# Value block means made in the second unit of a batch and spread by GpSimd, with a 192-byte head pitch in the value tile

## The chip, the cores and the metric

The kernel runs on one core of a Trainium2 chip. The metric is device time in microseconds, the median of three runs. The profile is one profiled execution of the same program. The engines are PE (matrix products; its weight loads are shown apart as PEld), DVE (VectorE), ACT (ScalarE), POOL (GpSimd) and SP (which here only issues DMAs). Each engine works through its own instructions in order; they wait for each other on semaphores.

## The reference, cut to what matters

Four batches of block-sparse attention (8 heads, 768 positions, 64 features a head) feed a gated feed-forward layer with a residual gate.

```python
k_sum = k.reshape(B, H, nb, block, D).max(axis=3)      # 24 blocks of 32 positions
v_sum = v.reshape(B, H, nb, block, D).mean(axis=3)
scores_l = scale * q @ k.T          # kept where |i - j| < 16, else -1e9
scores_s = scale * q @ k_sum.T + log(block)
a = softmax(concat([scores_l, scores_s], -1))
x = a @ concat([v, v_sum], axis=2)                     # to [3072, 512]
g = x @ w_gate;  val = x @ w_val
ffn = (gelu(g) * val) @ w_out
out = x + sigmoid(x @ w_res) * ffn
```

So every query sees the 31 nearest keys and, for each of 24 blocks, the maximum of its keys and the mean of its values. The change concerns these means, `v_sum`.

## The kernel before, in words

The work is cut into 8 units, two halves (`half` 0 and 1) of 384 positions for each of 4 batches. While unit u goes through the feed-forward layer, its tail computes the attention of unit u + 1, so PE always has matrix products of both. A unit has two parts:

- the **fo loop**, 12 steps: eight matmuls each into g and vv (PSUM pool `ps_mm`, four buffers), GELU on ACT, the product gvT on DVE (`fo_step`, L293);
- the **tail**: for the next unit four pairs of heads through scores (`s_step`), exponential, mask, and the attention-value product (`av_step`, matmuls `ao` at L273), then four transposes (`xt_step`), between the output matmuls f of the present unit (`ffn_step`), its residual gate (`res_step`) and its output (`end_step`, which sends `out` on SP).

The order is written out by hand (`tc.manual_schedule()`), so each engine executes in the order of the code.

**The value tile.** `vext[b % 2]` holds, for each of 12 windows of 64 queries (t) and each head, 128 rows of keys by 65 columns: rows 0 to 95 are the 96 positions around the window, rows 96 to 127 the block means, 24 of them used, the same for every t. Columns 0 to 63 are the values, column 64 is one (it gives the softmax sum). Values come in by 12 DMAs on POOL's queue (`v_loads`). The tile of batch b is that of batch b - 2, so two batches exist at a time.

**The block means of batches 1 to 3** go through four steps. `vsum_grp` (L229): 12 matmuls (L233) of the averaging matrix `bgrp` with the values of the 12 windows, into a PSUM tile `vs` in pool `ps_t`, tag "t", which has one buffer and is shared with the transposes of `xt_step` and, for batch 1, of `k_step` and `q_step`. DVE copies it to `vpart` (L237). SP sends four small DMAs (L239) that bring the groups of six rows to rows 96 to 119 of `vsum`. Last, `vsum_bc` (L242) copies the rows of `vsum` into rows 96 to 127 of three windows of `vext` at a time, so four copies fill a batch. Before the change the matmuls stand in the tail of the first unit of the batch before (L420, unit 0, 2 or 4), and the four copies are on DVE in fo steps 0 to 3 of the unit that follows (L383, unit 1, 3 or 5). The first `av_step` that needs them is in that unit's tail. Batch 0 has its own way at the start (`vsum_mm`, then one copy of six windows on DVE and one on POOL, L344 and L345), and it stays.

**What else stands on these queues.** POOL issues the loads of batch b + 1 at the start of unit 2b (L369): batch 1 by `load_qk` and `v_loads`, batches 2 and 3 by `load_nat` (12 DMAs for k_nat, 6 for q_nat) and `v_loads`. The instructions stand on POOL back to back, and at most eight of its DMAs are in flight; k_nat and q_nat have one buffer each. SP transposes them into kW and qT (`turn_all`, after fo step 6 of units 2 and 4). For batch 1, PE transposes the keys and queries instead, one pair of heads a step, in fo steps 2 to 9 of unit 1 (`k_step`, `q_step`). On DVE the block maxima of the keys (`k_blocks`, L198 and L202) follow: in unit 1 with `k_step`, in units 3 and 5 in fo steps 4 to 7.

Of the kernel before, what the change touches and what calls it, by code (L numbers as in the profile page):

```python
# [9 lines left out]
BF16 = mybir.dt.bfloat16  # L10
# [5 lines left out]
def kernel(  # L16
# [11 lines left out]
    nc = tc.nc  # L28
    B, H, S, D = q.shape
# [10 lines left out]
    NT = S // QT  # L40
    HT = NT // 2
# [5 lines left out]
    NQ = S // 128  # L47
    PJ = 8
    PP = S // PJ

    const = ctx.enter_context(tc.tile_pool(name="const", bufs=1))
    wpool = ctx.enter_context(tc.tile_pool(name="wpool", bufs=1))
# [7 lines left out]
    ps_t = ctx.enter_context(tc.tile_pool(name="ps_t", bufs=1, space=bass.MemoryType.PSUM))  # L60
# [9 lines left out]
    qT = [const.tile([128, NQ, NP, 128], BF16, name=f"qT{i}") for i in range(2)]  # L70
    k_nat = const.tile([BAND, NT, DM], BF16, name="k_nat")
    q_nat = const.tile([128, NQ, DM], BF16, name="q_nat")
    vext = [const.tile([128, NT, H, D + 1], BF16, name=f"vext{i}") for i in range(2)]
    vsum = [const.tile([128, DM], BF16, name=f"vsum{i}") for i in range(2)]
    vpart = const.tile([128, DM], BF16, name="vpart")
    w_gate = wpool.tile([128, KO, DFF], BF16, name="w_gate")
# [4 lines left out]
    def load_qk(src, b, parts, name):  # L81
        t = qk.tile([PP, H, PJ, D], BF16, tag=name, name=name)
        hs = H // parts
        for i in range(parts):
            nc.gpsimd.dma_start(
                out=t[:, i * hs:(i + 1) * hs].rearrange("p h j d -> p h (j d)"),
                in_=src[b, i * hs:(i + 1) * hs].rearrange("h (p j) d -> p h (j d)", j=PJ),
            )
        return t
# [7 lines left out]
    def v_loads(b):  # L97
        for t in range(NT):
            r0, r1, src = v_window(b, t)
            nc.gpsimd.dma_start(out=vext[b % 2][r0:r1, t, :, 0:D], in_=src)  # L100
# [13 lines left out]
    def turn_all(b):  # L114
        nc.sync.dma_start_transpose(out=kW[b % 2].rearrange("d t g k -> d (t g) k")[:, :, 0:BAND],
                                    in_=k_nat.rearrange("p t f -> p (t f)"))
        nc.sync.dma_start_transpose(out=qT[b % 2].rearrange("d c g k -> d (c g) k"),
                                    in_=q_nat.rearrange("p c f -> p (c f)"))

    with tc.manual_schedule():  # L120
# [66 lines left out]
        def turn_pair(src, hp, pool, tag):  # L187
            tp = pool.tile([128, PJ, PP], BF16, tag=tag, name="tp")
            for j in range(PJ):
                for hh in range(2):  # L190
                    nc.tensor.transpose(tp[hh * 64:hh * 64 + 64, j, :], src[:, 2 * hp + hh, j, :],
                                        ident[0:PP, 0:PP])
            return tp

        def k_blocks(b, hp):
            kw = kW[b % 2][:, :, hp]
            ks = work.tile([128, NB], BF16, tag="ks", name="ks")
            nc.vector.tensor_reduce(  # L198
                out=ks.rearrange("d (t n) -> d t n", n=2),
                in_=kw[:, :, WIN:WIN + QT].rearrange("d t (n w) -> d t n w", w=BLK),  # L200
                axis=mybir.AxisListType.X, op=ALU.max)
            nc.vector.tensor_copy(kw[:, :, BAND:BAND + NB], ks.unsqueeze(1).to_broadcast([128, NT, NB]))  # L202

        def k_step(b, hp, pool, tag):
# [3 lines left out]
            src = bass.AP(tensor=tp.tensor, offset=tp[:, 0, 6:7].offset,  # L208
                          ap=[tp[:].ap[0], [8, NT - 2], [1, 12], [PP, PJ]])
            nc.scalar.copy(kw[:, 1:NT - 1, 0:BAND].rearrange("d t (p j) -> d t p j", j=PJ), src)  # L210
            nc.vector.tensor_copy(kw[:, 0, WIN:BAND].rearrange("d (p j) -> d p j", j=PJ),
                                  tp[:, :, 0:10].rearrange("d j p -> d p j"))
            nc.vector.tensor_copy(kw[:, NT - 1, 0:BAND - WIN].rearrange("d (p j) -> d p j", j=PJ),
                                  tp[:, :, PP - 10:PP].rearrange("d j p -> d p j"))
            k_blocks(b, hp)
# [13 lines left out]
        def vsum_grp(b, pool, tag):  # L229
            vs = pool.tile([128, DM], F32, tag=tag, name="vs")  # L230
            for i in range(3):
                for g in range(4):
                    nc.tensor.matmul(vs[32 * g:32 * g + 32, :], bgrp[:, i, :],  # L233
                                     vext[b % 2][0:BAND, 3 * g + i, :, 0:D],
                                     start=(i == 0), stop=(i == 2), tile_position=(0, 32 * g),
                                     skip_group_check=True)
            nc.vector.tensor_copy(vpart[:], vs[:])  # L237
            for g in range(4):
                nc.sync.dma_start(out=vsum[b % 2][96 + 6 * g:102 + 6 * g, :],  # L239
                                  in_=vpart[32 * g:32 * g + 6, :])  # L240

        def vsum_bc(b, lo, hi, eng):  # L242
            src = vsum[b % 2][96:128, :].rearrange("p (h d) -> p h d", d=D)
            src = src.unsqueeze(1).to_broadcast([32, hi - lo, H, D])
            eng.tensor_copy(vext[b % 2][96:128, lo:hi, :, 0:D], src)  # L245
# [19 lines left out]
        def av_step(u, hp, st, pool=ps_o, tag="ao"):  # L265
            b, half = u // 2, u % 2
            P = st["P", hp]
            ao = pool.tile([128, NSUB, 2, D + 1], F32, tag=tag, name="ao")
            for sub in range(NSUB):
                for hh in range(2):  # L270
                    for e in range(2):
                        t = 2 * sub + e
                        nc.tensor.matmul(ao[64 * e:64 * e + 64, sub, hh, :], P[:, hh, t, :],  # L273
                                         vext[b % 2][:, half * HT + t, 2 * hp + hh, :],
                                         start=True, stop=True, skip_group_check=True)
            rz = work.tile([128, NSUB, 2, 1], F32, tag="rz", name="rz")
            nc.vector.reciprocal(rz[:], ao[:, :, :, D:D + 1])  # L277
            xn = st["xn"].rearrange("p s (h d) -> p s h d", d=D)[:, :, 2 * hp:2 * hp + 2, :]
            nc.vector.tensor_mul(xn, ao[:, :, :, 0:D], rz.to_broadcast([128, NSUB, 2, D]))  # L279
# [86 lines left out]
        for u in range(NU):  # L366
            b, half = u // 2, u % 2
            nb = b + 1
            if half == 0 and nb < B:  # L369
                if nb == 1:  # L370
                    k_sb[nb] = load_qk(k, nb, 1, "k_sb")
                    q_sb[nb] = load_qk(q, nb, 1, "q_sb")
                    v_loads(nb)
                else:
                    load_nat(nb)
                    v_loads(nb)
            gvT = upool.tile([128, FO, TU], BF16, tag="gvT", name="gvT")
            for fo in range(FO):
                fo_step(st, gvT, fo)
                if half == 0 and 1 < nb < B and fo == 6:  # L380
                    turn_all(nb)
                if half == 1 and nb < B:
                    if fo < 4:  # L383
                        vsum_bc(nb, 3 * fo, 3 * fo + 3, nc.vector)
                    if nb == 1:
                        if 2 <= fo < 2 + NP:
                            k_step(nb, fo - 2, ps_t, "t")
                        elif 2 + NP <= fo < 2 + 2 * NP:
                            q_step(nb, fo - 2 - NP, ps_t, "t")
                    elif 4 <= fo < 4 + NP:  # L390
                        k_blocks(nb, fo - 4)
            n = u + 1
            if n < NU:
                nst = new_unit()
                s_step(n, 0, nst)
            else:
                nst = None
            res_step(st, 0)
            ffn_step(st, gvT, 0, 0, FO)
            if nst:  # L400
                av_step(n, 0, nst)
                s_step(n, 1, nst)
            end_step(u, st, 0)
            res_step(st, 1)
            ffn_step(st, gvT, 1, 0, 4)
            if nst:
                av_step(n, 1, nst)
                s_step(n, 2, nst)
            ffn_step(st, gvT, 1, 4, FO)
            if nst:  # L410
                av_step(n, 2, nst)
                s_step(n, 3, nst)
                xt_step(n, 0, nst, ps_t, "t")
            end_step(u, st, 1)
            res_step(st, 2)
            ffn_step(st, gvT, 2, 0, 4)
            if nst:
                av_step(n, 3, nst)
                xt_step(n, 1, nst, ps_t, "t")
            if half == 0 and nb < B:  # L420
                vsum_grp(nb, ps_t, "t")
            ffn_step(st, gvT, 2, 4, FO)
            if nst:
                xt_step(n, 2, nst, ps_t, "t")
                xt_step(n, 3, nst, ps_mm, "mm")
            end_step(u, st, 2)
            st = nst
# [30 lines left out]
```

## Time and profile before

| | |
|---|---|
| time, median of 3 runs | 305.78 us (303.92 to 307.77) |
| profiled execution, span | 302.2 us |
| around the span, against the median | 3.6 us |
| PE busy | 263.6 us, 87% of the span |
| DVE / ACT / POOL busy | 171.8 / 124.8 / 89.9 us |
| mean matmuls L233, idle of PE before them | 10.6 us in all |
| four copies L245 on DVE, batches 1 to 3 | 12 of 952 ns |
| one copy L245 on POOL, batch 0 | 2744 ns for six windows |

The profiled execution's own time is not given apart from its span; what lies around the span is taken as the difference to the median of the runs. In a row of the groups the idle time is that of the engine just before the group's instructions, with what ended most of it behind an arrow. In a row of a timeline the first number is the start, the second the time that the row spans; x12 says that 12 instructions are merged, and square brackets give the idle time before and what ended it. Line numbers are those of the kernel before; behind the change they are one higher from line 50 on.

### The profile page before, as it was taken

How to read it: one execution, taken by the hardware profiler on the slowest of the kernel's cores; microseconds unless marked ns; L12 is line 12 of the kernel's file. 1: busy time of each engine (PE TensorE's matmuls, PEld its weight loads, DVE VectorE, ACT ScalarE, POOL GpSimd, SP SyncE). 2: the span in 40 equal slices, each digit the busy share in tenths (PEclk: the TensorE clock that was granted, in tenths of full speed). 3: DMA queues.
4: the chain of work that ended last, by engine and by line, in shares of the span. 5: the costliest groups of instructions: out<-in, count | busy, mean ns of one | idle time of the engine just before them, and what ended most of it. 6: DMA issues, size and time to landing. Idle time of an engine off the chain costs nothing.

```text
span 302.2 us, 5706 instructions
## 1 busy us (share of the span) xinstructions
PE 263.6 (87%) x2307; PEld 144.4 (48%) x2330; DVE 171.8 (57%) x373; ACT 124.8 (41%) x188; POOL 89.9 (30%) x127
## 2 busy tenths in 40 slices
PE   1666999927889999997979999997999999999994
PEld 0623565502445455543535456553554556455641
DVE  3545643630994475447497584366994754475423
ACT  2652535420356643364224443543336433643310
POOL 7977683278970000579700000000000000000000
PEclk9978699985999999999999999999999999999999
DMA  6999999999999017999990019501100100010001
GB/s 102 167 101 187 196 206 207 165 158 134 155 116 52 0 72 144 173 122 171 161 44 2 35 37 198 100 35 38 38 2 0 69 37 2 1 72 35 2 36 69
DMA packets 98122, 27.51 MB, mean 91 GB/s; under 512 B 83688, under 2 KB 95024, under 8 KB 98096
## 3 DMA queue, kind: packets, MB, share of 16 engines
q0 software_dynamic: 79008, 16.85, 92.3%
q1 hardware_dynamic: 19088, 10.30, 13.4%
q8 instruction: 18, 0.29, 0.4%
q14 instruction: 8, 0.07, 0.1%
HBM read 33.69 MB, written 6.29 MB: 132 GB/s over the span
## 4 chain that ended last, share of the span: by engine, by line
PE 64%; DMA 13%; DVE 12%; issue 4%; ACT 3%; POOL 1%; SPq 1%; DVEq 0%; POOLq 0%
PE f L321 17%; PE g L297 16%; PE vv L301 15%; DMA q_sb<-in_q_dram 8%; PE r L311 6%; DVE vext L245 3%; DVE gvT L305 3%; PE ao L273 3%; DMA vext<-in_v_dram 3%; PE s L255 3%; DMA vsum<-vpart 3%; DVE ks L198 2%; PE xp L284 2%; SPq L239 1%; PE wp L342 1%
## 5 line engine op out<-in xcount | busy, mean ns | idle before, releaser
L304 ACT ACTIVATE ge<-g 128x384 f32<-128x384 f32 x96 | 47.2, 491 | 104.9 <-PE g L297 63.7
L297 PE MATMUL g<-xT,w_gate 128*128 128x384 bf16 x384 | 81.0, 331 | 1.6 <-DVE gvT L305 1.6
L301 PE MATMUL vv<-xT,w_val 128*128 128x384 bf16 x384 | 78.7, 328 | 1.7 <-DVE gvT L305 0.8
L305 DVE TENSOR_TENSOR gvT<-ge,vv 128x384 bf16<-128x384 f32 x96 | 52.6, 551 | 48.0 <-PE vv L301 47.6
L321 PE MATMUL f<-w_out,gvT 128*128 128x512 bf16 x274 | 66.9, 386 | 2.0 <-issue 1.8
L301 PEld LDWEIGHTS <-w_val 128*128 128x128 bf16 x384 | 37.7, 98 | 29.2 <-issue 5.5
L297 PEld LDWEIGHTS <-w_gate 128*128 128x128 bf16 x384 | 37.2, 99 | 26.7 <-issue 4.4
L321 PEld LDWEIGHTS <-gvT 128*128 128x128 bf16 x288 | 27.5, 99 | 34.0 <-issue 3.7
L259 ACT ACTIVATE P<-s,bias_t 128x768 bf16<-128x768 f32 x32 | 28.9, 903 | 34.2 <-PE s L255 34.1
L100 POOL DMA_DIRECT2D vext<-in_v_dram x48 | 36.6, 778 | 16.4 <-DMA w_out<-in_moe_w_out_dram 4.3
L262 DVE TENSOR_TENSOR P<-P,maskt 128x768 bf16<-128x768 bf16 x32 | 17.7, 554 | 21.2 <-ACT P L259 21.2
L108 POOL DMA_DIRECT2D k_nat<-in_k_dram x24 | 18.1, 762 | 36.8 <-DMA kW<-k_nat 32.9
L311 PE MATMUL r<-w_res,xT 128*128 128x512 bf16 x88 | 24.4, 381 | 0.4
L326 DVE SCALAR_TENSOR_TENSOR th<-th,f 128x512 f32<-128x512 f32 x24 | 16.3, 679 | 7.0 <-PE f L321 7.0
L279 DVE TENSOR_TENSOR xn<-ao,rz 128x384 bf16<-128x384 f32 x32 | 17.8, 557 | 1.1
L314 ACT ACTIVATE th<-r 128x512 f32<-128x512 f32 x24 | 14.3, 595 | 8.8 <-PE r L311 8.3
L328 DVE SCALAR_TENSOR_TENSOR o<-th,xn 128x512 f32<-128x512 f32 x24 | 16.6, 692 | 0.8
L273 PEld LDWEIGHTS <-P 128*64 128x64 bf16 x384 | 8.9, 113 | 14.4 <-DVE P L262 5.9
L198 DVE TENSOR_REDUCE ks<-kW 128x24 bf16<-128x768 bf16 x16 | 15.2, 949 | 0.3
L277 DVE RECIPROCAL rz<-ao 128x6 f32<-128x6 f32 x32 | 6.1, 192 | 15.7 <-PE ao L273 15.6
L245 DVE COPY vext<-vsum 32x1536 bf16<-32x1536 bf16 (+1 forms) x13 | 12.4, 952 | 4.1 <-DMA vsum<-vpart 3.8
L255 PE MATMUL s<-qT,kW 64*128 64x64 bf16 x384 | 11.4, 194 | 3.2 <-ACT P L259 3.2
(72 smaller groups left out, 177.7 us busy)
## 6 DMA issues: line engine op xcount, KB each, us to landing
out_dram<-o SPq DMA_DIRECT2D x24, 256.0 KB
vext<-in_v_dram POOLq DMA_DIRECT2D x40, 96.0 KB, 7.4
k_nat<-in_k_dram POOLq DMA_DIRECT2D x20, 96.0 KB, 5.4
w_gate<-in_moe_w_gate_dram POOLq DMA_DIRECT2D x6, 256.0 KB, 8.9
w_val<-in_moe_w_val_dram POOLq DMA_DIRECT2D x6, 256.0 KB, 9.2
w_out<-in_moe_w_out_dram POOLq DMA_DIRECT2D x3, 512.0 KB, 13.9
q_nat<-in_q_dram POOLq DMA_DIRECT2D x12, 128.0 KB, 5.8
k_sb<-in_k_dram POOLq DMA_DIRECT2D x2, 384.0 KB, 5.5
```

Of the source, the lines that this page charges most:

```text
L100: nc.gpsimd.dma_start(out=vext[b % 2][r0:r1, t, :, 0:D], in_=src)
L108: nc.gpsimd.dma_start(out=k_nat[r0:r0 + hi - lo, t].rearrange("p (h d) -> p h d", d=D), in_=k[b, :, lo:hi, :].rearrange("h p d -> p h d"))
L198: nc.vector.tensor_reduce(out=ks.rearrange("d (t n) -> d t n", n=2), in_=kw[:, :, WIN:WIN + QT].rearrange("d t (n w) -> d t n w", w=BLK), ...
L245: eng.tensor_copy(vext[b % 2][96:128, lo:hi, :, 0:D], src)
L255: nc.tensor.matmul(s[:, hh, t * QT:(t + 1) * QT], kw[ps, tt, hp, :], qt[ps, tt // 2, hp, (tt % 2) * QT:(tt % 2 + 1) * QT], start=True, sto ...
L259: nc.scalar.activation(P.rearrange("p a t q -> p a (t q)"), s[:, :, 0:TU], AF.Exp, scale=scale, bias=bias_t[:])
L297: nc.tensor.matmul(g[:, 0:TU], w_gate[:, ko, fs], st["xT"][:, ko, :], start=(ko == 0), stop=(ko == KO - 1))
L301: nc.tensor.matmul(vv[:, 0:TU], w_val[:, ko, fs], st["xT"][:, ko, :], start=(ko == 0), stop=(ko == KO - 1))
L304: nc.scalar.activation(ge[:], g[:, 0:TU], AF.Gelu)
L305: nc.vector.tensor_mul(gvT[:, fo, :], ge[:], vv[:, 0:TU])
L311: nc.tensor.matmul(r[:], st["xT"][:, ko, ss], w_res[:, ko, :], start=(ko == 0), stop=(ko == KO - 1))
L321: nc.tensor.matmul(st["f"][:], gvT[:, fo, ss], w_out[:, fo, :], start=(fo == 0), stop=(fo == FO - 1))
```

## The change

Three things change.

1. The value tile's last dimension is 96 instead of 65 elements, so that the rows of one head and window start 192 bytes after those of the one before, where it was 130. The matmuls of `av_step` read columns 0 to 64 of it, as before. Loads and copies move the same elements.
2. `vsum_grp` for the next batch moves out of the tail of units 0, 2 and 4, into the fo loop of the unit behind: after step 10 of unit 1 for batch 1, after step 0 of units 3 and 5 for batches 2 and 3. Its vpart copy on DVE and its four DMAs on SP go with it.
3. The four copies of `vsum_bc` follow directly behind `vsum_grp` in the code, and on POOL instead of DVE.

```diff
+    VP = 96
...
-    vext = [const.tile([128, NT, H, D + 1], BF16, name=f"vext{i}") for i in range(2)]
+    vext = [const.tile([128, NT, H, VP], BF16, name=f"vext{i}") for i in range(2)]
...
-                                         vext[b % 2][:, half * HT + t, 2 * hp + hh, :],
+                                         vext[b % 2][:, half * HT + t, 2 * hp + hh, 0:D + 1],
...
                 if half == 1 and nb < B:
-                    if fo < 4:
-                        vsum_bc(nb, 3 * fo, 3 * fo + 3, nc.vector)
+                    if fo == (10 if nb == 1 else 0):
+                        vsum_grp(nb, ps_t, "t")
+                        for i in range(4):
+                            vsum_bc(nb, 3 * i, 3 * i + 3, nc.gpsimd)
...
-            if half == 0 and nb < B:
-                vsum_grp(nb, ps_t, "t")
             ffn_step(st, gvT, 2, 4, FO)
```

On DVE, at the border of units 2 and 3 (batch 2), before the change: xT are the transposes' copies of the tail, th and o the output, gvT the first steps of the fo loop.

```order
L286 COPY xT<-xp 128x384
L237 CAST vpart<-vs 128x512
L286 COPY xT<-xp 128x384 x2
L326 SCALAR_TENSOR_TENSOR th<-th,f 128x512
L328 SCALAR_TENSOR_TENSOR o<-th,xn 128x512
L305 TENSOR_TENSOR gvT<-ge,vv 128x384
L245 COPY vext_97<-vsum_99 32x24x64
L305 TENSOR_TENSOR gvT<-ge,vv 128x384
```

The same place with the change:

```order
L287 COPY xT<-xp 128x384 x3
L327 SCALAR_TENSOR_TENSOR th<-th,f 128x512
L329 SCALAR_TENSOR_TENSOR o<-th,xn 128x512
L306 TENSOR_TENSOR gvT<-ge,vv 128x384
L238 CAST vpart<-vs 128x512
L306 TENSOR_TENSOR gvT<-ge,vv 128x384 x4
L199 TENSOR_REDUCE ks<-kW_91 128x24
L203 COPY kW_91<-ks 128x12x24
```

vpart has moved from between the transposes' copies to behind the first gvT, and the copies into vext between the gvT are gone from DVE; the key maxima follow where they did.

On POOL, where the loads of batch 1 (vext_98) end and those of batch 2 (k_nat, q_nat, vext_97) begin, before:

```order
L100 DMA vext_98<-in_v_dram 96x8x64 x10
L100 DMA vext_98<-in_v_dram 80x8x64
L108 DMA k_nat<-in_k_dram 80x8x64
L108 DMA k_nat<-in_k_dram 96x8x64 x10
L108 DMA k_nat<-in_k_dram 80x8x64
L111 DMA q_nat<-in_q_dram 128x8x64 x6
```

and with the change:

```order
L101 DMA vext_98<-in_v_dram 96x8x64 x10
L101 DMA vext_98<-in_v_dram 80x8x64
L246 COPY vext_98<-vsum_100 32x24x64 x4
L109 DMA k_nat<-in_k_dram 80x8x64
L109 DMA k_nat<-in_k_dram 96x8x64 x10
L109 DMA k_nat<-in_k_dram 80x8x64
L112 DMA q_nat<-in_q_dram 128x8x64 x6
```

The four copies of batch 1, which wait for the four DMAs of its means, now stand ahead of the 30 loads of batch 2. In the same way batch 2's copies stand ahead of batch 3's loads.

## The prediction

> **What bounds the kernel now.** I read the page's busy shares first (PE is by far the busiest engine), then PE's timeline, and cut the span where each unit's first g matmul (L297) starts. The view of stages, with those cuts, has a row for each of units 0 to 6: start and end, length, busy time (and count) of PE, PEld, DVE, ACT and POOL, then the granted clock, the DMA share and GB/s:
>
> ```profile
> 32.14:75.56 43.42, 35.37 (x263) 18.13 (x265) 17.86 (x51) 15.51 (x23) 26.83 (x37) 0.85 2.09 176
> 75.56:112.71 37.15, 34.52 (x380) 19.02 (x381) 26.29 (x54) 20.20 (x29) 13.86 (x18) 0.99 1.73 78
> 112.71:144.95 32.24, 30.32 (x264) 16.66 (x265) 17.25 (x35) 13.75 (x21) 17.97 (x23) 1.00 1.46 155
> 144.95:178.48 33.53, 30.45 (x253) 16.29 (x253) 24.20 (x46) 13.75 (x21) 5.47 (x8) 1.00 0.79 52
> 178.48:210.72 32.24, 30.32 (x264) 16.66 (x265) 17.25 (x35) 13.75 (x21) 0.00 (x0) 1.00 0.41 89
> 210.72:241.61 30.89, 30.15 (x252) 16.31 (x253) 24.20 (x46) 13.75 (x21) 0.00 (x0) 1.00 0.07 25
> 241.61:271.36 29.75, 29.49 (x253) 16.34 (x253) 16.55 (x34) 13.74 (x21) 0.00 (x0) 1.00 0.08 28
> ```
>
> Unit 6 has nothing of a next batch in it: 29.75 us, PE busy for 29.49. That is the floor of a unit. Units 0, 2 and 4 hold the mean matmuls (L233) in their tails, units 1, 3 and 5 the spreading copies (L245). PE's timeline at the ends of units 0, 2 and 6:
>
> ```profile
> 61.16 0.34 PE L284 MATMUL xp<-ident,xn 128*128 128x128 bf16 x3
> 63.05 0.40 PE L233 MATMUL vs<-vext,bgrp 96*32 96x512 bf16 x2 [1.55 <-DVE xT L286]
> ...
> 68.73 0.62 PE L233 MATMUL vs<-vext,bgrp 96*32 96x512 bf16 x4 [2.81 <-DMA vext<-in_v_dram]
> ...
> 71.94 3.19 PE L321 MATMUL f<-w_out,gvT 128*128 128x512 bf16 x7 [0.33 <-issue]
> ...
> 142.11 0.84 PE L233 MATMUL vs<-vext,bgrp 96*32 96x512 bf16 x12 [1.55 <-DVE xT L286]
> 143.11 1.67 PE L321 MATMUL f<-w_out,gvT 128*128 128x512 bf16 x7 [0.16 <-issue]
> ...
> 239.37 0.34 PE L284 MATMUL xp<-ident,xn 128*128 128x128 bf16 x3
> ```
>
> In unit 0 PE stands in order before the mean matmuls until batch 1's values land (about 71.9); in unit 2 the values are there, but the matmuls wait 1.55 for the one PSUM buffer "t" that xT's copy frees.
>
> **The change, unit by unit.** All times are on this profile's clock.
>
> Unit 0, tail. Without the mean matmuls the tail is unit 6's: from the last xp before them to the next g 241.61 - 239.37 = 2.24 us, in place of 75.56 - 61.16 = 14.40. Gain 12.16; unit 1 starts at 63.40. Its key and query tiles are there by then:
>
> ```profile
> 41.85 16.76 DMA q_sb<-in_q_dram
> ```
>
> Unit 1. Now its fo loop loses four DVE copies and gains the mean matmuls after step 10. PE before:
>
> ```profile
> 79.99 0.53 PE L191 MATMUL tp<-ident,k_sb 96*64 96x96 bf16 x16
> ...
> 88.08 0.53 PE L191 MATMUL tp<-ident,k_sb 96*64 96x96 bf16 x16 [0.16 <-DVE kW L213]
> 90.10 0.53 PE L191 MATMUL tp<-ident,q_sb 96*64 96x96 bf16 x16
> ...
> 98.87 0.35 PE L255 MATMUL s<-qT,kW 64*128 64x64 bf16 x12
> ```
>
> First key step 79.99 - 75.56 = 4.43 after the start; four key steps at 2.02 (90.10 - 88.08, the interval without a spreading copy) are 8.08, against 10.11 now; from there to the scores (s) 8.77 as now, and 1.00 for the mean matmuls (142.11 to 143.11, no wait: values in by 71.9, needed at about 83). So s comes 22.28 after the unit's start, now 23.31.
>
> The chain mean matmuls, vpart, four small DMAs, copies, attention-value matmuls (ao) is now inside 12 us. Its rows:
>
> ```profile
> 143.06 0.69 DVE L237 CAST vpart<-vs 128x512 bf16<-128x512 f32 x1 [1.01 <-PE vs L233]
> 150.52 0.95 DVE L245 COPY vext<-vsum 32x1536 bf16<-32x1536 bf16 x1 [3.12 <-DMA vsum<-vpart]
> 208.83 0.69 DVE L237 CAST vpart<-vs 128x512 bf16<-128x512 f32 x1 [1.01 <-PE vs L233]
> 213.65 0.95 DVE L245 COPY vext<-vsum 32x1536 bf16<-32x1536 bf16 x1 [0.49 <-DMA vsum<-vpart]
> 164.64 0.35 PE L255 MATMUL s<-qT,kW 64*128 64x64 bf16 x12
> 168.48 0.38 PE L273 MATMUL ao<-vext,P 128*64 128x65 bf16 x12
> 36.00 2.74 POOL L245 COPY vext<-vsum 32x3072 bf16<-32x3072 bf16 x1
> ```
>
> From vpart's end to the first copy 4.13 us with the DMA queues quiet (213.65 - 209.52), 6.77 with loads in flight (150.52 - 143.75). I take 4.13: batch 2's loads now stand behind the copies on POOL, so nothing else moves. The mean matmuls end at 22.28 - 1.33 (step 11; 15.92 / 12 from unit 6 below) = 21.0 after the unit's start, vpart's 0.69 ends at 21.8, and the first copy starts at 25.9. One GpSimd copy of 32x3072 took 2.74; a copy of half is 1.37 by size alone, 2.74 if the time were fixed. I take 1.42. The first ao matmuls need two copies: ready at 28.75, due at 22.28 + 3.84 = 26.1. **New stall of PE: 2.65 us**, with end_step and the next scores queued behind it.
>
> A stall of this length also costs clock. Three stretches of 3.41 us:
>
> ```profile
> 59.35:62.77 3.42, 2.15 (x23) 1.02 (x21) 2.92 (x8) 2.39 (x3) 2.54 (x4) 1.00 4.39 107
> 62.77:66.18 3.41, 0.77 (x3) 0.19 (x3) 0.23 (x1) 0.00 (x0) 2.68 (x5) 1.00 2.20 177
> 66.18:69.60 3.42, 0.62 (x4) 0.11 (x4) 0.00 (x0) 0.00 (x0) 2.34 (x4) 0.50 2.80 157
> ```
>
> After 0.77 of 3.41 busy the clock fell to 0.50; after 2.15 it had not. A stall of 2.65 leaves as little as 0.76 in a stretch. The price is in the tail of unit 0: 3.62 from f to g (71.94 to 75.56), against 1.84 (143.11 to 144.95): 1.78. If the clock is set by stretches with fixed borders, the stall would have to fall about evenly on two of them for it to hold; I take 3 in 4 for the fall, and so it is in the sum. [...]
>
> The unit's tail without stalls is 112.71 - 98.87 = 13.84. Unit 1: 22.28 + 13.84 + 2.65 + 1.78 = 40.55, now 37.15: loss 3.40; unit 2 starts at 103.95.
>
> Units 2 and 4 lose the mean matmuls and become unit 6: 32.24 - 29.75 = 2.49 each.
>
> Units 3 and 5. The mean matmuls come after step 0, where "t" is long free, and the DVE copies go:
>
> ```profile
> 227.77 0.35 PE L255 MATMUL s<-qT,kW 64*128 64x64 bf16 x12
> 257.53 0.35 PE L255 MATMUL s<-qT,kW 64*128 64x64 bf16 x12
> ```
>
> From g to s: unit 6 15.92, unit 5 17.05, unit 3 19.69, since in unit 3 DVE waited 3.12 for the vsum DMA with gvT queued behind and PE ran out of PSUM. That wait is POOL's now, with only loads behind it. 15.92 + 1.00 + 0.1 (four key reductions remain on DVE) = 17.0. Unit 3: 17.0 + 13.84 = 30.84, gain 2.69; unit 5 gains 0.05. Here the copies have room: mean matmuls end 2.3 after the start, two copies are ready by 2.3 + 0.8 + 6.77 + 2.84 = 12.7 at worst, ao due at 20.8.
>
> What moves on POOL: batch 2's 30 loads (k_nat, q_nat, v) went from 63.71 to 91.20 and now start behind four copies, at 63.40 + 25.9 + 5.7 = 95.0:
>
> ```profile
> 63.71 1.61 POOL L108 DMA_DIRECT2D k_nat<-in_k_dram  x2
> 90.48 0.72 POOL L100 DMA_DIRECT2D vext<-in_v_dram  x1 [0.23 <-issue]
> 115.42 5.97 SPq L115 DMA_TRANSPOSE kW<-k_nat  x1
> 121.67 3.61 SPq L117 DMA_TRANSPOSE qT<-q_nat  x1
> vext<-in_v_dram POOLq DMA_DIRECT2D x40, 96.0 KB, 7.4
> ```
>
> 27.5 us of issue end at 122.5, the last values land by 129.9 (7.4), unit 3 needs them at 103.95 + 29.75 + 1.3 = 135.0. Slack 5.1, the cover of this move. SP's transposes start when k_nat is in, near 110, and end by 125; needed at step 4 of unit 3. Batch 3 has over 10 us of slack in the same sum.
>
> The head pitch changes no count of bytes, issues or copies. Its bounds are the v loads' 7.4 halved or doubled: at 3.7 the slack above grows, at 14.8 the values land 2.3 after they are needed, inside the rival of late values below. The row itself says 7.4, so I take zero.
>
> **Sum:** -12.16 + 3.40 - 2.49 - 2.69 - 2.49 - 0.05 = -16.5. Span 302.2 - 16.5 = 285.7. The median is 305.78, 3.6 above the span; with the same around it, 289.3.
>
> **Rivals.**
> *Shorter stall* (0.13): the clock holds, 289.3 - 1.8 = 287.5, and copies under 1.37 at the new pitch could take the rest of the stall, 284.9. About 287.
> *Copies cost the same whatever their size* (0.08):
>
> ```profile
> L245 DVE COPY vext<-vsum 32x1536 bf16<-32x1536 bf16 x12 | 11.4, 952 | 4.1 <-DMA vsum<-vpart 3.8
> L245 DVE COPY vext<-vsum 32x3072 bf16<-32x3072 bf16 x1 | 1.0, 959 | 0.0
> ```
>
> DVE did so: 952 ns for half of 959 ns. If GpSimd does, two copies are 5.5 instead of 2.84: 292. Against it: two engines need not share that.
> *Late values* (0.10): transposes and loads take turns. All 9.9 us of 115.42 to 125.28 added to 129.9 gives 139.8 against 135.0: 4.8 more, 294.
> *GpSimd and DVE block each other* (0.05): each copy stops DVE for its length, four of them 5.7 us in each of units 3 and 5. DVE has idle time in a step (1.33 less the 0.55 of gvT), which would take up part; at most all of 11.4 shows, 300.7, which is within 2%. In unit 0 a gvT multiplication ran beside the 2.74 copy and took 0.56, about the mean of its line, 551 ns:
>
> ```profile
> 36.65 0.56 DVE L305 TENSOR_TENSOR gvT<-ge,vv 128x384 bf16<-128x384 f32 x1 [1.08 <-PE vv L301]
> ...
> L305 DVE TENSOR_TENSOR gvT<-ge,vv 128x384 bf16<-128x384 f32 x96 | 52.6, 551 | 48.0 <-PE vv L301 47.6
> ```
>
> [...]
> *Slower* (0.03): the copies take C each, so long that the loads behind them on POOL come late too. The stall in unit 1 is 2C - 0.2. Batch 2's values land at 124.2 + 4C (129.9 at 1.42) and are needed at 132.15 + 2C: from C = 4.0 the mean matmuls of unit 3 wait, and each us costs 4. Batch 3's loads start behind four more copies and have 60.6 us from mean matmuls to mean matmuls for 40.7 + 4C: from C = 5.0 each us costs 8. That makes 285.7 + 2 x 2.58 + 4 = 294.9 of span at C = 5, level with now at C = 5.9, and at C = 7 a time of 314.5. It decides at four times the row's 1.37, and nothing in the trace shows GpSimd that slow.
>
> **Numbers.** The forecast has 0.61. Predicted 289.3. The range runs from 285 (no stall, clock held) to 295 (late values at 294, and a little for the spread of the runs); the last two rivals, 0.08 together, lie outside. About 2% (6.1 us) is what a measurement can tell from no change. Faster by more: 0.61 + 0.13 + 0.08 + 0.10 = 0.92. Within: 0.05. Slower: 0.03.
>
> **What would show it.** Right: f follows xp within 0.5 us at the end of unit 0; unit 1 about 40.5 with PE's ao waiting some 2.7 us for GpSimd; units 2 and 4 at 29.75, 3 and 5 near 30.8; copies near 1.4 us. Wrong: mean matmuls waiting for v in unit 3, copies over 2.7 us, DVE lines longer beside them, or PE waiting for v at step 10 of unit 1.

## The result, and the profile after

| | before | with the change |
|---|---|---|
| time, median | 306.3 us (303.92 to 307.77) | 294.49 us (290.06 to 297.83) |
| ratio | 1 | 0.953, 95% interval 0.942 to 0.963 |
| profiled execution, span | 302.2 us | 291.1 us |
| forecast: time, ratio, span | | 289.3 us (285 to 295), 0.946, 285.7 us |

The change makes the kernel 4.7% faster. The ratio is that of the faster executions, 290.06 and 292.99 us for the change; its two slower ones, 295.98 and 297.83, count in the median alone. Direction and range held; the span is 5.4 us longer than the sum. The profiled execution took 292.99 us, 1.9 above its span, and the runs of the kernel before that were made for the experiments lie 1.7 to 1.8 above theirs. So only about half of the 3.6 that the prediction put around the span lies around it; the rest was the spread of the runs, and the sum is judged by the span.

The view of stages of the kernel with the change, units 0 to 5, cut where each unit's first g matmul starts, with the columns of the same view of before:

```profile
33.02:64.11 31.09, 31.09 (x255) 16.87 (x254) 16.74 (x49) 15.51 (x23) 15.17 (x22) 0.95 1.51 194
64.11:104.20 40.09, 37.16 (x396) 19.63 (x393) 24.07 (x51) 20.20 (x29) 14.33 (x16) 0.96 0.36 37
104.20:133.94 29.74, 29.74 (x256) 16.33 (x253) 16.55 (x34) 13.74 (x21) 14.81 (x19) 1.00 1.79 156
133.94:168.56 34.62, 33.27 (x267) 17.12 (x265) 21.97 (x43) 13.75 (x21) 25.20 (x29) 0.95 1.34 101
168.56:198.30 29.74, 29.74 (x255) 16.33 (x253) 16.55 (x34) 13.76 (x21) 3.98 (x6) 1.00 0.99 130
198.30:230.53 32.23, 30.87 (x267) 16.46 (x265) 23.20 (x43) 13.74 (x21) 5.70 (x4) 1.00 0.07 26
```

Units 0, 2 and 4 are what the sum said: 31.09, 29.74, 29.74 for 31.26, 29.75, 29.75. Unit 1 is 40.09 for 40.55. Units 3 and 5 are not: 34.62 and 32.23, both for 30.84. Unit 7 is as before. So the 5.4 is 0.9 ahead of unit 0 (the start moved from 32.14 to 33.02; it lay anywhere from 31.4 to 33.1 in the runs below), -0.2 in unit 0, -0.5 in unit 1, **3.8 in unit 3 and 1.4 in unit 5**.

PE's timeline with the change, at the tail of unit 0, the tail of unit 1, the start of unit 3, and unit 5:

```profile
61.87 0.34 PE L285 MATMUL xp<-ident,xn 128*128 128x128 bf16 x3
62.05 1.89 PE L322 MATMUL f<-w_out,gvT 128*128 128x512 bf16 x8
...
91.39 0.26 PE L274 MATMUL ao<-vext,P 128*64 128x65 bf16 x5 [1.37 <-POOL vext L246]
92.80 0.29 PE L274 MATMUL ao<-vext,P 128*64 128x65 bf16 x7 [1.16 <-POOL vext L246]
...
136.75 0.40 PE L234 MATMUL vs<-vext,bgrp 96*32 96x512 bf16 x4 [0.81 <-DMA vext<-in_v_dram]
137.54 0.84 PE L234 MATMUL vs<-vext,bgrp 96*32 96x512 bf16 x5 [0.39 <-DMA vext<-in_v_dram]
...
212.06 0.81 PE L302 MATMUL vv<-xT,w_val 128*128 128x384 bf16 x4 [1.36 <-DVE gvT L306]
```

f follows xp at once at the end of unit 0, where 10.8 us lay between them before. In unit 1 PE waits 1.37 + 1.16 = 2.53 for the copies; 2.65 was forecast. Two waits were not in the sum: in unit 3 the mean matmuls wait for values (1.20), and in unit 5 a vv waits 1.36 for gvT.

POOL's timeline with the change: batch 1's copies, the end of batch 2's loads, batch 3's copies:

```profile
89.87 5.70 POOL L246 COPY vext<-vsum 32x1536 bf16<-32x1536 bf16 x4 [29.12 <-DMA vsum<-vpart]
...
120.81 0.77 POOL L101 DMA_DIRECT2D vext<-in_v_dram  x1 [3.99 <-PE s L256]
...
125.59 2.42 POOL L101 DMA_DIRECT2D vext<-in_v_dram  x3 [2.42 <-PE r L312]
...
205.76 5.70 POOL L246 COPY vext<-vsum 32x1536 bf16<-32x1536 bf16 x4 [32.19 <-DMA vsum<-vpart]
```

Four copies take 5.70, 1.425 each, as taken (1.42). But POOL stops among the value loads, and issues the last at about 128.0, where the sum had 122.5. The releasers named there (s and r of PE) have nothing to do with a load. In this trace never more than eight of POOL's DMAs are in flight, and the issues at 120.81, 122.40 and 125.59 start 0.55 to 0.57 after the load eight before them has landed (120.24, 121.85 and 125.04). So these are waits for a place among the eight. What was slow beside them is seen on SP, whose two transposes took 5.97 and 3.61 before:

```profile
109.62 9.37 SPq L116 DMA_TRANSPOSE kW<-k_nat  x1
120.39 9.10 SPq L118 DMA_TRANSPOSE qT<-q_nat  x1
```

The last of these loads, from issue to landing, in the view of the critical chain:

```profile
127.29 10.67 DMA vext<-in_v_dram
```

It lands at 137.96; 129.9 was forecast.

DVE's timeline with the change, in unit 1's tail and in unit 5, while POOL copies (from 205.76 in steps of 1.425: copies end at 207.2, 208.6, 210.0 and 211.5):

```profile
94.34 1.64 DVE L263 TENSOR_TENSOR P<-P,maskt 128x768 bf16<-128x768 bf16 x1 [0.43 <-ACT P L260]
...
207.61 1.12 DVE L203 COPY kW<-ks 128x288 bf16<-128x288 bf16 x1
208.65 0.53 DVE L306 TENSOR_TENSOR gvT<-ge,vv 128x384 bf16<-128x384 f32 x1
209.11 0.94 DVE L199 TENSOR_REDUCE ks<-kW 128x24 bf16<-128x768 bf16 x1
210.08 1.47 DVE L203 COPY kW<-ks 128x288 bf16<-128x288 bf16 x1
...
212.91 0.24 DVE L203 COPY kW<-ks 128x288 bf16<-128x288 bf16 x1
```

The copy of the key maxima (L203) takes 0.24 alone. Started inside a POOL copy, it ends when that one does: 208.73 against 208.6, 211.55 against 211.5. gvT, which reads PSUM, keeps its 0.53 in the same stretch, and so does the reduction of the maxima (L199), which reads and writes SBUF: 0.94, where its mean was 0.95 before.

### The profile page after: what moved, and what is told of

Same layout as the page of the kernel before. It is cut to its first block, busy times and chain, and to the rows that moved or that the text cites. A ratio compares the mean times of both kernels' runs of the same rounds, so it can differ in the third digit from the quotient of the medians.

```text
span 291.1 us, 5733 instructions
## 1 busy us (share of the span) xinstructions
PE 265.4 (91%) x2330; PEld 144.3 (50%) x2330; DVE 163.4 (56%) x361; ACT 124.8 (43%) x188; POOL 106.6 (37%) x139
## 4 chain that ended last, share of the span: by engine, by line
PE 78%; DVE 7%; DMA 7%; issue 3%; ACT 3%; POOL 1%; SPq 1%; POOLq 0%; DVEq 0%
PE g L298 20%; PE f L322 19%; PE vv L302 19%; PE r L312 7%; DMA vext<-in_v_dram 4%; PE ao L274 3%; PE s L256 3%; DVE ks L199 2%; DMA q_sb<-in_q_dram 2%; PE xp L285 2%; DVE gvT L306 2%; PE wp L343 2%; PE tp L192 1%; ACT qT L220 1%; ACT kW L211 1%
## 5 line engine op out<-in xcount | busy, mean ns | idle before, releaser
L322 PE MATMUL f<-w_out,gvT 128*128 128x512 bf16 x288 | 69.5, 383 | 0.0
L246 POOL COPY vext<-vsum 32x1536 bf16<-32x1536 bf16 (+1 forms) x13 | 19.8, 1564 | 76.7 <-DMA vsum<-vpart 76.7
L322 PEld LDWEIGHTS <-gvT 128*128 128x128 bf16 x288 | 27.5, 98 | 31.7 <-issue 1.1
L263 DVE TENSOR_TENSOR P<-P,maskt 128x768 bf16<-128x768 bf16 x32 | 18.9, 590 | 22.1 <-ACT P L260 22.0
L274 PE MATMUL ao<-vext,P 128*64 128x65 bf16 x384 | 12.6, 203 | 4.5 <-POOL vext L246 2.5
L199 DVE TENSOR_REDUCE ks<-kW 128x24 bf16<-128x768 bf16 x16 | 15.2, 948 | 0.3
## 6 DMA issues: line engine op xcount, KB each, us to landing
q_nat<-in_q_dram POOLq DMA_DIRECT2D x12, 128.0 KB, 5.4
```

Of the source, the lines that this page charges most:

```text
L199: nc.vector.tensor_reduce(out=ks.rearrange("d (t n) -> d t n", n=2), in_=kw[:, :, WIN:WIN + QT].rearrange("d t (n w) -> d t n w", w=BLK), ...
L263: nc.vector.tensor_mul(Pf, Pf, maskt.unsqueeze(1).to_broadcast([128, 2 * HT, QT]))
L322: nc.tensor.matmul(st["f"][:], gvT[:, fo, ss], w_out[:, fo, :], start=(fo == 0), stop=(fo == FO - 1))
```

## The experiments

The lengths of the units, cut in the same way in every kernel's trace (us):

| kernel | start | 0 | 1 | 2 | 3 | 4 | 5 | 6 | 7 | span |
|---|---|---|---|---|---|---|---|---|---|---|
| before | 32.14 | 43.42 | 37.15 | 32.24 | 33.53 | 32.24 | 30.89 | 29.75 | 30.84 | 302.2 |
| forecast | 32.14 | 31.26 | 40.55 | 29.75 | 30.84 | 29.75 | 30.84 | 29.75 | 30.84 | 285.7 |
| the change | 33.02 | 31.09 | 40.09 | 29.74 | 34.62 | 29.74 | 32.23 | 29.74 | 30.83 | 291.1 |
| pitch alone | 32.49 | 36.25 | 37.81 | 33.91 | 30.46 | 32.23 | 30.88 | 29.74 | 30.83 | 294.6 |
| change, old pitch | 31.44 | 30.87 | 40.14 | 29.75 | 37.28 | 29.75 | 32.25 | 29.75 | 30.87 | 292.1 |
| means after step 6 | 32.22 | 31.11 | 37.18 | 29.74 | 30.61 | 29.74 | 30.61 | 29.74 | 30.75 | 281.7 |
| step 6 for batches 2, 3 | 32.92 | 31.20 | 40.08 | 29.74 | 30.61 | 29.74 | 30.61 | 29.74 | 30.76 | 285.4 |
| no transposes | 33.03 | 31.10 | 40.08 | 29.75 | 32.12 | 29.74 | 32.31 | 29.75 | 31.02 | 288.9 |
| values loaded first | 31.48 | 30.97 | 40.09 | 29.74 | 32.29 | 29.74 | 32.24 | 29.75 | 30.80 | 287.1 |
| twelve small copies | 32.18 | 30.69 | 40.70 | 29.74 | 32.41 | 29.74 | 30.61 | 29.74 | 30.79 | 286.6 |
| warm PE in unit 1 | 32.81 | 31.40 | 39.56 | 29.74 | 36.06 | 29.75 | 32.23 | 29.74 | 30.81 | 292.1 |
| step 6, own PSUM | 33.02 | 31.38 | 35.48 | 29.74 | 30.61 | 29.74 | 30.61 | 29.74 | 30.78 | 281.1 |
| step 6, old pitch | 33.08 | 31.17 | 37.21 | 29.75 | 30.62 | 29.75 | 30.63 | 29.75 | 30.84 | 282.8 |

The kernels that have no ratio below were executed once, so only their units are read. How far two executions can differ shows in unit 3 of the kernel with a warm PE in unit 1: it has the change's own code there, and yet 36.06 for 34.62, since PE waited 2.49 for the values and not 1.20.

My theory after the result: unit 3 is late values, slowed by the transposes that now run beside their loads, with a slower clock behind the wait; unit 5 is DVE held by POOL's copies. The rivals: that the loads simply start too late behind the copies; that the new pitch slows something; that the wait in unit 5 is the longer DVE queue (vpart) and not a hold.

### The pitch alone

The kernel before, with the new pitch only:

```diff
+    VP = 96
...
-    vext = [const.tile([128, NT, H, D + 1], BF16, name=f"vext{i}") for i in range(2)]
+    vext = [const.tile([128, NT, H, VP], BF16, name=f"vext{i}") for i in range(2)]
...
-                                         vext[b % 2][:, half * HT + t, 2 * hp + hh, :],
+                                         vext[b % 2][:, half * HT + t, 2 * hp + hh, 0:D + 1],
```

> The kernel before, with the 192-byte head pitch alone. Theory: the pitch only shortens the value loads (the median to landing falls from 7.4 towards 5.5 us), so the mean matmuls of unit 0 wait less for them; units 1 to 7 keep their lengths within 0.3 us. Unit 0 falls from 43.4 by 0 to 4 us, ratio to before 0.985 to 1.0. Rival: the gain of the whole change comes largely from the pitch; then the ratio is near 0.96 and unit 0 near 33.

297.98 us beside 305.12, ratio 0.975 (0.970 to 0.980): a larger gain than expected. Unit 0 is 36.25 for 43.42, and units 1 to 3 didn't keep their lengths. Unit 3 gains 3.1, since DVE's first copy there no longer waits for the DMA of vsum (3.12 before). Units 1 and 2 give 2.3 back, 1.7 of it in unit 2, where the granted clock was 0.50 from 136.88 to 140.29. PE's timeline at the end of unit 0, and POOL's with batch 2's value loads:

```profile
63.86 1.20 PE L234 MATMUL vs<-vext,bgrp 96*32 96x512 bf16 x9 [0.72 <-DMA vext<-in_v_dram]
65.22 3.19 PE L322 MATMUL f<-w_out,gvT 128*128 128x512 bf16 x7 [0.16 <-issue]
```

```profile
74.68 9.17 POOL L101 DMA_DIRECT2D vext<-in_v_dram  x12
```

In the kernel before POOL needed longer for the same twelve loads, from 80.22 to 91.20, with a wait ahead of nearly each of the last six. From its timeline, and the row of the DMA issues of the kernel with the pitch alone:

```profile
80.22 4.63 POOL L100 DMA_DIRECT2D vext<-in_v_dram  x6
85.31 0.77 POOL L100 DMA_DIRECT2D vext<-in_v_dram  x1 [0.46 <-PE vv L301]
```

```profile
vext<-in_v_dram POOLq DMA_DIRECT2D x40, 96.0 KB, 4.9
```

The median load lands in 4.9 us where it took 7.4. So PE waits 0.72 for batch 1's values, where before it waited 5.95 in four pieces, 2.81 the longest. The pitch is not free of effect: in this order of the loads the value loads were faster with it. The tail of unit 0 still pays for the clock (0.50 from 66 to 68 us; f in 3.19, as before).

### The change with the old pitch

```diff
-    VP = 96
+    VP = D + 1
```

> The change without its pitch: mean matmuls moved, copies on GpSimd, 130-byte pitch. Theory: units 0, 2, 4, 5 and 6 as with the whole change (31.1, 29.7, 29.7, 32.2, 29.7); copies near 1.43 us; unit 3 waits longer for batch 2's values, since these loads are slower at this pitch (1.2 us of DMA waits with the pitch, 2 to 5 without), so unit 3 is 35 to 39 and the ratio to before 0.955 to 0.97. Rival: the pitch does nothing; then unit 3 is 34.6 and the ratio 0.953.

295.97 us beside the same 305.12, ratio 0.968 (0.963 to 0.973). All units but one agree with the change within 0.3; unit 3 is 37.28 instead of 34.62. PE's timeline there:

```profile
135.75 0.40 PE L234 MATMUL vs<-vext,bgrp 96*32 96x512 bf16 x4 [1.54 <-DMA vext<-in_v_dram]
137.01 1.12 PE L234 MATMUL vs<-vext,bgrp 96*32 96x512 bf16 x5 [0.86 <-DMA vext<-in_v_dram]
```

The row of the DMA issues, first of the change and then of this kernel:

```profile
vext<-in_v_dram POOLq DMA_DIRECT2D x40, 96.0 KB, 5.8
```

```profile
vext<-in_v_dram POOLq DMA_DIRECT2D x40, 96.0 KB, 8.2
```

Between these two traces the pitch is worth 2.7 us of unit 3. About half of that could be the difference between two executions: with a warm PE, at the new pitch, unit 3 is 36.06, the two ratios' intervals touch, and the median landing was 6.4 with the warm PE and 8.0 with the twelve small copies, which load in the change's order. Alone the pitch gave 7.6 us of span: it shortens the same wait that the move of the mean matmuls takes out of unit 0, so the two gains don't add up. Nothing here makes the new pitch a cause of the lost time.

### The means after step 6, for all batches

```diff
-                    if fo == (10 if nb == 1 else 0):
+                    if fo == 6:
```

> The change with the mean matmuls and the four copies after step 6 of units 1, 3 and 5, in place of 10, 0 and 0. Theory: the values of batch 2 have 8 us more, so unit 3 has no wait before the mean matmuls and no fall of the clock behind one; the GpSimd copies run after the block maxima in units 3 and 5, so the DVE copies of the maxima are back at 0.23 us; in unit 1 the copies are ready before the ao matmuls. Unit 1 falls from 40.1 to 35.5 to 36.5, units 3 and 5 to 30.6 to 31.2; the span to about 281, ratio to before 0.92 to 0.935. Rival (unit 5 is long because of the block maxima themselves, whatever runs on GpSimd): unit 5 stays near 32.2.

284.26 us beside 305.12, ratio 0.930 (0.926 to 0.934). Units 3 and 5 in the view of stages:

```profile
130.25:160.86 30.61, 30.35 (x264) 16.48 (x265) 21.84 (x43) 13.73 (x21) 15.01 (x17) 1.00 0.48 48
190.60:221.21 30.61, 30.35 (x264) 16.48 (x265) 21.77 (x43) 13.73 (x21) 6.02 (x4) 1.00 0.18 42
```

That is the floor of a unit and twelve mean matmuls: 29.74 + 0.87. The 30.84 of the prediction was right as a term; in the change, two causes lie on top of it. Of the 4.01 that unit 3 of the change has over this, 2.0 lie ahead of its second g, with the 1.20 of waits in them: that g starts 4.37 after the unit's start, and 2.38 in the kernel below that loads the values first. Another 1.7 lie right behind it, where the granted clock was 0.50 from 138.41 to 141.82: the next three groups of four matmuls took 3.63 there and 1.96 in that kernel, at 1.00.

Unit 1 lost its stall for the copies, but came out at 37.18, above what was expected, for a new reason in PE's timeline and DVE's:

```profile
77.92 0.53 PE L192 MATMUL tp<-ident,q_sb 96*64 96x96 bf16 x16 [1.44 <-DVE vpart L238]
```

```profile
77.18 0.68 DVE L238 CAST vpart<-vs 128x512 bf16<-128x512 f32 x1
```

The query transposes of batch 1 need the one PSUM buffer "t" that vs holds until DVE, busy with the key maxima, has copied it.

### Step 6 for batches 2 and 3 only

```diff
-                    if fo == (10 if nb == 1 else 0):
+                    if fo == (10 if nb == 1 else 6):
```

> The same move to step 6, in units 3 and 5 alone; unit 1 keeps step 10. Theory: unit 1 stays at 40.1 with its stall of 2.5 us for GpSimd and the fall of the clock, units 3 and 5 are 30.6 to 31.2. So the move's gain splits into about 4.5 in unit 1 (by difference to the run with step 6 everywhere) and about 5 in units 3 and 5. Rival: batch 3's loads, which now start 8 us later, come late to unit 5; then PE waits for values in unit 5 and it is above 32.

Span 285.4. Unit 1 stays at 40.08, units 3 and 5 are both 30.61. The place of batch 1's means sets unit 1 alone, that of the others units 3 and 5: the 4.0 and 1.6 us lost there belong to "after step 0". By difference, step 6 wins 2.9 in unit 1 and not the 4.5 expected, for the wait of 1.44 takes part of it back. It doesn't tell late values from held DVE, since a later place cures both.

### No transposes

```diff
                 if half == 0 and 1 < nb < B and fo == 6:
-                    turn_all(nb)
+                    pass
```

> The change without the two pairs of DMA transposes of keys and queries (batches 2 and 3 use old keys and queries, so this part of the computation is left out). Theory: batch 2's value loads are late in unit 3 because they share the DMA engines with the transposes; without these, POOL issues its 30 loads in 24 to 25 us (33 with them, with waits of 4.0, 0.8 and 2.4 us), the mean matmuls of unit 3 wait for no values, the clock does not fall there, and unit 3 is 30.6 to 32.3 in place of 34.6. Rival: they are late only because they start behind the GpSimd copies, at 95.5; then POOL's waits and unit 3's length stay.

Unit 3 is 32.12; the mean matmuls wait for nothing there. POOL's timeline and PE's:

```profile
110.47 4.62 POOL L101 DMA_DIRECT2D vext<-in_v_dram  x6
115.43 4.57 POOL L101 DMA_DIRECT2D vext<-in_v_dram  x6 [0.33 <-issue]
```

```profile
135.57 0.83 PE L234 MATMUL vs<-vext,bgrp 96*32 96x512 bf16 x12
147.61 0.81 PE L302 MATMUL vv<-xT,w_val 128*128 128x384 bf16 x4 [1.35 <-DVE gvT L306]
```

The loads start where they did in the change and are all issued by 120.0, instead of 128.0. So a late start behind the copies is not enough; it is the transposes in the same stretch. And with the values in time, unit 3 shows the wait of unit 5, 1.35 for gvT.

### The values ahead of keys and queries

```diff
-                    load_nat(nb)
                     v_loads(nb)
+                    load_nat(nb)
```

> The change with the value loads of batches 2 and 3 ahead of the key and query loads on POOL. Theory: the values are in by about 110, before the transposes start, so unit 3 has no wait for them and no fall of the clock: 30.8 to 32.3. The key and query loads end 9 us later, their transposes near 138; the block maxima in unit 3 need them at about 141, so nothing new waits. Rival: the transposes come late; then DVE waits for kW in unit 3 and it stays above 33.

Span 287.1, unit 3 32.29. All computation is there, transposes included, only the order on POOL's queue differs. PE's timeline in unit 3:

```profile
133.89 0.83 PE L234 MATMUL vs<-vext,bgrp 96*32 96x512 bf16 x12
...
146.10 0.81 PE L302 MATMUL vv<-xT,w_val 128*128 128x384 bf16 x4 [1.36 <-DVE gvT L306]
```

No wait for values, and again the wait for gvT. Taking the late values away thus wins 34.62 - 32.29 = 2.3. It also uncovers the wait for gvT, which the change's unit 3 didn't have; what is left to 30.61 is 1.7.

### Twelve copies of one window

```diff
-                        for i in range(4):
-                            vsum_bc(nb, 3 * i, 3 * i + 3, nc.gpsimd)
+                        for i in range(NT):
+                            vsum_bc(nb, i, i + 1, nc.gpsimd)
```

> The change with 12 GpSimd copies of one window each in place of 4 of three windows, for each batch. [...] A copy is now 0.5 to 0.6 us, so no kW copy in unit 5 takes more than 0.9, the sum of its excess falls from 2.1 to below 1.3 us, and PE's wait of 1.36 in unit 5 falls below 0.7. The 12 copies together are 6 to 7.5 us, up from 5.7. [...]

The bound of 0.9 is an estimate from the change's trace: 0.24 for the copy of the key maxima alone, and at most one whole POOL copy, since a L203 that started inside one ended within 0.1 us of its end there. Unit 5 is 30.61, and the wait for gvT is gone. POOL's and DVE's timelines there:

```profile
202.92 6.78 POOL L246 COPY vext<-vsum 32x512 bf16<-32x512 bf16 x12 [29.89 <-DMA vsum<-vpart]
```

```profile
204.76 0.53 DVE L203 COPY kW<-ks 128x288 bf16<-128x288 bf16 x1
```

POOL works longer (6.78 for 5.70), so more of its work lies beside DVE's, and yet the four L203 have 0.5 us in all over 0.23 each, where they had 2.1: the longest took 0.53, so none was held for longer than one copy of 0.57. So the loss goes with the length of a single copy (1.425 and 0.57 were tried), and vpart, which DVE has in this kernel too, is not the cause. In unit 1, whose ao waits for the copies, the twelve take 7.10 in all, and the unit is 0.6 longer than in the change. Unit 3 is 32.41 for 34.62, though PE still waits 0.60 and 0.45 for values there: the granted clock stayed at 1.00 behind these waits (the next four g in 0.82), where it fell behind the 0.81 and 0.39 of the change (1.40). What else differs in these 2.2 us was not taken apart.

### A warm PE in unit 1

Ten matmuls of a tile without use, ahead of the attention-value matmuls that stall:

```diff
+                if u == 1:
+                    wp = ps_t.tile([128, 512], F32, tag="t", name="wp")
+                    for i in range(10):
+                        nc.tensor.matmul(wp[:], warm[:, 0:128], warm[:], start=True, stop=True)
                 av_step(n, 0, nst)
```

> The change with ten additional matmuls of zeros, 2.2 us of work for PE, in unit 1 ahead of the first ao matmuls, where PE waits 2.5 us for GpSimd. Theory: the wait also lets the granted clock fall to half for some 3 us behind it; with PE busy through most of it the clock stays at 1.00 and unit 1 falls from 40.1 by 1.0 to 1.8, while the GpSimd copies end when they did. Rival: the time behind the wait is lost to DVE (the held mask multiplication), not to the clock; then unit 1 keeps its 40.1.

The clock held: the granted clock from 94 to 96 us was 0.51 in the change, first, and 1.00 here, second, in the view of stages:

```profile
94.00:96.00 2.00, 2.00 (x6) 0.50 (x4) 1.66 (x2) 0.91 (x2) 2.00 (x3) 0.51 0.00 0
```

```profile
94.00:96.00 2.00, 1.30 (x6) 0.39 (x4) 1.57 (x2) 1.01 (x2) 2.00 (x3) 1.00 0.00 0
```

But unit 1 is only 0.53 shorter, 39.56. PE's timeline says why:

```profile
92.90 0.29 PE L274 MATMUL ao<-vext,P 128*64 128x65 bf16 x7 [0.41 <-POOL vext L246]
...
96.14 0.38 PE L274 MATMUL ao<-vext,P 128*64 128x65 bf16 x12 [0.83 <-DVE P L263]
```

The second pair's ao starts at 96.14 in both kernels, since the mask multiplication (L263, 1.64 in both, against a mean of 0.55 before) is held by the last copy. The slow clock hid a second delay of nearly its own size.

### Step 6, and a PSUM buffer of its own

The kernel with step 6 for all batches, and batch 1's vs in the pool of the feed-forward products:

```diff
-                        vsum_grp(nb, ps_t, "t")
+                        vsum_grp(nb, *((ps_mm, "mm") if nb == 1 else (ps_t, "t")))
```

> Step 6 everywhere, and for batch 1 the mean matmuls write into a buffer of the pool of g and vv in place of the one buffer t. Theory: with t, PE's next query transposes wait 1.44 us in unit 1 until DVE, busy with the block maxima, has copied vpart; with another buffer they do not. Unit 1 falls from 37.2 to 35.7 to 36.0, all else as with step 6, span near 280.3, ratio to before 0.92 to 0.93. Rival: vpart's buffer is then missing for g and vv two steps later, and the wait moves there; unit 1 stays above 36.8.

282.76 us beside 305.15, ratio 0.925 (0.920 to 0.930). PE's timeline in unit 1:

```profile
76.53 0.83 PE L234 MATMUL vs<-vext,bgrp 96*32 96x512 bf16 x12
77.29 0.53 PE L192 MATMUL tp<-ident,q_sb 96*64 96x96 bf16 x16
```

The query transposes follow without a wait and unit 1 is 35.48. This is the fastest of all kernels here. Against the one with step 6 alone it is 1.7 us shorter in unit 1; the ratios' intervals overlap.

### Step 6 with the old pitch

The kernel with step 6 for all batches, and `VP = D + 1`.

> Step 6 everywhere, with the 130-byte pitch of before. Theory: the pitch saves time only where PE stands waiting for values; with the mean matmuls at step 6 none of them waits, so units 1 to 7 have the lengths of the 192-byte run within 0.3 us, and the ratio to before is 0.925 to 0.94, as there. Rival: the pitch also helps elsewhere (reads by PE, copies); then it is slower by 1% or more, above 0.94.

284.36 us beside 305.15, ratio 0.930 (0.924 to 0.936), and every unit within 0.1 of the same kernel with the new pitch, whose ratio is 0.930 too. Where the values are in time, the pitch is worth nothing that these runs show.

## Why the prediction was right, and where it was wrong

**Unit 0 and units 2 and 4** were right to 0.2 us: the tail without the mean matmuls is unit 6's. (The row at 239.37, read as the end of unit 6, is that of unit 5; unit 6's own, at 269.12, gives the same 2.24.)

**Unit 1** was right in each piece: scores 22.00 after the start (22.28), stall 2.53 (2.65), copies 1.425 (1.42), and the clock fell. What the unit has beyond these is 40.09 - (22.00 + 13.84) - 2.53 = 1.72, for the 1.78 put on the clock; but the warm PE won only 0.53: two delays lie on top of each other there, and the held mask multiplication was in the sum at nothing. That the clock fell, to 0.51 from 94 to 96 us, after a stall of 2.53, in two pieces, goes with the trace's row of 0.77 busy, though 1.50 of the 3.41 us ahead of this fall were busy (last section).

**The step that failed is "Slack 5.1, the cover of this move".** It took the issue of 30 loads at its length before, 27.5, and 7.4 for the last landing. In the kernel before the transposes ran long after the loads; in the change they run beside them. The prediction's own times had the two side by side, transposes from 110 to 125 and issue from 95.0 to 122.5, but each at its length alone. Issue ended near 128.0 instead of 122.5 and the last load took 10.67 instead of 7.4: the values were in 8 us later, at 137.96, and the cover was 5.1. The rival "late values" named this mechanism, with a price of 4.8. Unit 3 lost 3.8; taking the lateness away wins 2.3 (values first) to 2.5 (no transposes), since the hold of DVE then shows. The waits that the trace names are only 1.20 of the loss: PE's clock fell behind them for 3.4 us (last section).

**"Units 3 and 5 ... 17.0"** put what stands beside the copies at nothing. The rival "GpSimd and DVE block each other" (0.05) was real, in part: not each copy stopped DVE for its length, but the key maxima's copy and the mask product, started during a POOL copy, took up to 1.47 for 0.24 and 1.64 for 0.55, and ended 0.1 and 0.4 us behind that copy (the mask product at 95.98, the copy at 95.57); the reduction and gvT kept their 0.94 and 0.53. It cost 1.6 in unit 5, 1.5 to 1.7 in unit 3 where the values were in time, and it was hidden in unit 3 of the change, whose copies came late with the values: there PE waited for no gvT. The line means of before and of the change carry it; gvT's, which the prediction went by, doesn't: 551 ns before, 552 in the change. From the groups of before, then of the change:

```profile
L202 DVE COPY kW<-ks 128x288 bf16<-128x288 bf16 x16 | 4.4, 273 | 0.6
```

```profile
L203 DVE COPY kW<-ks 128x288 bf16<-128x288 bf16 x16 | 7.0, 437 | 0.5
```

**The pitch at zero** was wrong, and its bound was right: the landing at "halved or doubled" 7.4 held 4.9 and 5.8. A row of one pitch can't say what another does. Units 0 to 7 of the change with the old pitch are 7.1 above the sum, those of the change 4.5, so the pitch hid part of the same failed step, as far as one trace of each can tell. Why it helped is not settled: only 130 and 192 bytes were tried.

**The numbers.** The sum missed the span by 5.4, of which 4.5 are units 0 to 7. That the time fell inside the range is in part luck: its upper end stood for late values alone, at 4.8, of which 3.8 came, and the 1.4 of unit 5, which nothing in it stood for, happened to fit beneath it. "Copies cost the same whatever their size" and "slower" are out by the 1.425.

## What to carry to other kernels

When loads are moved behind something, look at what they will run beside, not only at when they end: here the last load took 10.67 us beside the transposes, where 7.4, the median in the old place, was the price. When a copy moves to GpSimd, list the DVE instructions that will start during it. Here the key maxima's copy and the mask product lost up to 1.2 and 1.1 us beside copies of 1.425, the reduction and gvT nothing; copies of 0.57 (0.3 and 0.5 at most), or a place behind the key maxima (unit 5 in 30.61 for 32.23), cost less. Then try the place of the step as a number of its own: from steps 10 and 0 to step 6 the span fell by 9.4 us, with no instruction changed.

## What the runs showed of the hardware that was not expected

**The granted clock changed at whole numbers of 3.413 us, and the busy share alone didn't decide.** In the change it fell at 94.04 and at 138.41, and came back 3.4 us later each time; the distance of 44.37 is 13 times 3.413. In the kernel before it fell at 66.19 and came back at 76.43, 10.24 later, 3 times 3.413. In these two traces every change of the granted clock within the span lies a whole number of 3.413 us from the others. The stretches of 3.41 ahead of the two falls, in the view of stages:

```profile
90.63:94.04 3.41, 1.50 (x28) 0.96 (x28) 0.75 (x2) 0.63 (x1) 3.41 (x3) 1.00 0.00 0
135.00:138.41 3.41, 2.16 (x17) 0.58 (x16) 1.34 (x3) 0.49 (x1) 0.00 (x0) 1.00 1.21 233
```

It fell after 2.16 us busy, as much as the 2.15 after which it held in the rows of before. The second stretch is largely mean matmuls, of 32 columns; whether these count for less was not tried. In the kernel with the pitch alone two such stretches, each with the twelve mean matmuls in it, are still closer, and the clock fell behind the first (f in 3.19 there) and held behind the second (f in 1.67):

```profile
133.46:136.88 3.42, 1.76 (x29) 0.88 (x29) 2.36 (x6) 1.40 (x2) 2.92 (x4) 1.00 2.25 145
198.32:201.73 3.41, 1.70 (x29) 0.86 (x23) 2.34 (x6) 0.93 (x1) 0.00 (x0) 1.00 0.20 77
```

What decides between them stays open.

**Transposes and POOL's loads slowed each other.** The two transposes took 5.97 and 3.61 apart from the loads, 9.37 and 9.10 beside them, and POOL's last six loads took 12.0 us to issue (116.05 to 128.0) instead of the 4.57 without transposes. In the kernel that loads the values first, the second transpose, behind the last issue (117.7), took 4.06.

**The head pitch of the destination.** With 192 bytes for 130 the same bytes landed sooner: 7.4 to 4.9 us (median) in the order of before, 8.2 to 5.8 in that of the change, 13.1 to 11.2 with step 6. Only the direction is common to the three: the kernels that have the new pitch and the change's order of loads range from 5.8 to 8.0.
